# Top-32 attention and a mixture of depths on one core: the 32nd score found from a bound and an exact count, with a general way behind a branch

## The chip, the core and the metric

The program runs on one core of one Trainium2 chip. A core has a matmul engine (PE, whose weight loads are listed as PEld), a vector engine (DVE), an activation engine (ACT), a general engine (POOL) and a queue engine that issues most DMAs (SP). The metric is the device time of one execution in microseconds (us), the median of several runs.

## The reference

The inputs are fixed: the reference draws them after seeding its generator with 0. There are 8 batches, 8 heads, 576 tokens and 64 values per head.

```python
scores = scale * np.matmul(q, k.transpose(0, 1, 3, 2))          # scale = 1/8
kth = np.partition(scores, -32, axis=-1)[..., -32:-31]
scores = np.where(scores >= kth, scores, -1000000000.0)
attn = np.exp(scores - np.max(scores, axis=-1, keepdims=True))
attn = attn / (np.sum(attn, axis=-1, keepdims=True) + 1e-09)
x = np.matmul(attn, v)                       # -> (batch, token, 8 heads * 64 = 512)
# mixture of depths, per batch
s = x @ w_gate
top = the 128 tokens of the highest s
out = x;  out[top] = x[top] + sigmoid(s[top]) * (relu(x[top] @ w1) @ w2)
```

Each of the 8 x 8 x 576 = 36,864 rows of scores has 576 scores, and its 32nd greatest decides which scores count.

## The kernel before

**Tiles and units.** The queries of a head lie in four full tiles of 128 rows and a last one of 64. The work is cut into 160 units, 20 to a batch: a pair of heads (`hp`, 0 to 3) on a tile of queries (`t`, 0 to 4). A unit with `t` below 4 has two score tiles of 128 rows, one per head. A unit with `t` = 4 has one score tile that holds both heads' 64 rows. So there are 288 score tiles, each 128 rows by 576 scores.

**One unit.** `scores` multiplies on PE into PSUM (`ps`) and ACT copies the products to `sc`. `top_k` finds the 32nd score on DVE in four rounds: each round takes the 8 greatest (MAX8, tiles `first` and `best`), and between rounds a MATCH_REPLACE8 (with a small MATCH_VALUE_LOAD ahead of it) strikes them out into `left`. `weigh` makes `shift` on POOL, the exponentials `e` on ACT, a mask with the 32nd score on POOL and the product `p` on POOL. `turn` transposes `p` on PE (tiles `ptr` and `small`), ACT copies that to `pT`. `values` multiplies `pT` with `v` on PE into another part of `small`; a column of ones in `v` gives the sum of the weights. ACT copies the result to `xs`. After the four pairs of heads of a tile, `normalise` divides (DVE, then POOL writes `x`) and `gates` makes the tokens' gate scores (DVE, tile `prod`).

**Mixture.** When a batch's attention is done, `mixture` ranks its tokens (`tied`, on DVE), picks 128 with one-hot matmuls (`xe_ps`, `extra_ps`), runs the two layers (`h_ps`, `y_ps`) and adds the result to `out` with an indirect DMA that POOL issues. It is a generator; one step of it goes into each unit of the next batch.

**Order.** The order on PE, DVE, ACT and POOL is the order in which the code is written: the class `InOrder` records every operation of the main loop, so that nearly all of them carry line 33 in the profile, and they are told apart by tiles. The loop runs over n. While DVE does `top_k` for unit n, PE makes the scores of n + 1, the values of n - 2, and turns the weights of n - 1. The loads of q, k and v of the next batch (`load_qkv`, eight steps of transposes on PE and copies on ACT) go between the last units of a batch; SP issues their DMAs.

Of the kernel before, what the change touches and what calls it, by code (L numbers as in the profile page):

```python
# [15 lines left out]
# Below every score: what match_replace puts in place of the values already taken.  # L16
LOWEST = -3.0e38
TOP_K = 32
CAP = 128
# Full tiles of 128 tokens; token 4 * p + j sits on partition p of tile j, so that  # L20
# a partition's four tokens are contiguous in memory. The last 64 tokens are tile J.
# [3 lines left out]
class InOrder:  # L25
    """An engine whose instructions stay in the order in which they are written."""
# [10 lines left out]
def kernel(  # L37
# [29 lines left out]
    ldpool = ctx.enter_context(tc.tile_pool(name="ld", bufs=2))  # L67
    kqpool = ctx.enter_context(tc.tile_pool(name="kq", bufs=2))
    scpool = ctx.enter_context(tc.tile_pool(name="sc", bufs=6))
    wkpool = ctx.enter_context(tc.tile_pool(name="wk", bufs=4))  # L70
    stats = ctx.enter_context(tc.tile_pool(name="stats", bufs=12))
    ppool = ctx.enter_context(tc.tile_pool(name="p", bufs=3))
    ptpool = ctx.enter_context(tc.tile_pool(name="pt", bufs=4))
# [11 lines left out]
    # The place of each token in its sequence, and the row of slots 0 .. CAP-1.  # L85
# [8 lines left out]
    # before[p, t, c] = 1 where the token of column c comes before token (p, t):  # L94
    # of tokens with the same gate score, the earlier one is taken first.
# [24 lines left out]
    # v with a column of ones: the product with it is the softmax's denominator.  # L120
# [22 lines left out]
    def room_for_qkv(b):  # L143
        """q and k transposed, [(h d), pair of heads, token]; v as [token, head, tile, d]."""
        qT = kqpool.tile([P, NHP, S], FP32, name="qT")
        kT = kqpool.tile([P, NHP, S], FP32, name="kT")
        return qT, kT, vbufs[b % 2]

    def load_qkv(b, qT, kT, vt):
        """In 2 * NHP steps, k and q of a pair of heads; each asks for the next one's rows."""  # L150

        def fetch(src, hp, name):
            rows = ldpool.tile([P, NT, 2, D], FP32, name=name)
            for hh in range(2):
                nc.sync.dma_start(
                    out=rows[:, 0:J, hh, :],
                    in_=src[b, 2 * hp + hh, 0:JP, :].rearrange("(p j) d -> p j d", j=J),
                )
            nc.sync.dma_start(
                out=rows[0:R, J, :, :],  # L160
                in_=src[b, 2 * hp : 2 * hp + 2, JP:S, :].rearrange("h p d -> p h d"),
            )
            return rows
# [4 lines left out]
            for src, dst, name in ((k, kT, "kin"), (q, qT, "qin"))  # L168
        ]
        fetched = {}  # L170
        for i, (src, dst, hp, name) in enumerate(todo):
# [5 lines left out]
            for c in range(J):  # L177
# [15 lines left out]
                in_=v[b, i, 0:JP, :].rearrange("(p j) d -> p j d", j=J),  # L193
            )
            nc.sync.dma_start(out=vt[0:R, i, J, 0:D], in_=v[b, i, JP:S, :])
            yield

    def top_k(scs):
        """Of each tile's rows, the greatest score and the least of the TOP_K greatest."""
        cur, left, first = list(scs), {}, {}  # L200
        for r in range(TOP_K // 8):
            best = {}
            for i in range(len(scs)):
                best[i] = stats.tile([P, 8], FP32, name="best" if r else "first")
                dve.max(best[i], cur[i])
            first = first or best
            if r < TOP_K // 8 - 1:
                for i in range(len(scs)):
                    if r == 0:
                        left[i] = wkpool.tile([P, S], FP32, name="left")  # L210
                    dve.match_replace(left[i], best[i], cur[i], LOWEST)
                    cur[i] = left[i]
        return [(first[i][:, 0:1], best[i][:, 7:8]) for i in range(len(scs))]

    def heads_of(t):
        """Of each score tile of a pair of heads: its heads and their first rows.

        Rows of a score tile are queries: of one head in a full tile, and of both
        heads, one below the other, in the last tile.
        """  # L220
        return [[(0, 0), (1, R)]] if t == J else [[(0, 0)], [(1, 0)]]

    def scores(t, hp, qT, kT):
        """The pair's score tiles; two heads' products go to banks of their own."""
# [11 lines left out]
        scs = []  # L236
        for ps in pss:
            sc = scpool.tile([P, S], FP32, name="sc")
            act.copy(
                out=sc.rearrange("p (u s) -> p u s", u=2), in_=ps[:, :, 0:HALF]  # L240
            )
            scs.append(sc)
        return scs

    def weigh(scs, tops):
        """exp(scale * (score - greatest)) where a score is among its row's TOP_K, else 0."""
        weights = []
        for sc, (top, kth) in zip(scs, tops):
            shift = stats.tile([P, 1], FP32, name="shift")
            pool.tensor_scalar_mul(shift, top, -scale)  # L250
            e = ppool.tile([P, S], FP32, name="e")
            act.activation(e, sc, AF.Exp, bias=shift, scale=scale)
            p = ppool.tile([P, S], FP32, name="p")
            pool.tensor_scalar(
                out=p, in0=sc, scalar1=kth, scalar2=None, op0=ALU.is_ge
            )
            pool.tensor_tensor(p, p, e, ALU.mult)
            weights.append(p)
        return weights

    def turn(weights):
        """The weights transposed, [key, chunk of keys, query]."""
        small = ps_small.tile([P, 512], FP32, name="small")
        turned = []
        for i, p in enumerate(weights):
            pT = ptpool.tile([P, NT, P], FP32, name="pT")
            tr = ps_tr.tile([P, 512], FP32, name="ptr")
            for c in range(J):
                pe.transpose(
                    tr[:, c * P : (c + 1) * P], p[:, c * P : (c + 1) * P], ident  # L270
                )
            pe.transpose(small[0:R, i * P : (i + 1) * P], p[:, JP:S], ident)
            act.copy(
                out=pT[:, 0:J, :], in_=tr.rearrange("p (c i) -> p c i", c=J)
            )
            act.copy(out=pT[0:R, J, :], in_=small[0:R, i * P : (i + 1) * P])
            turned.append(pT)
        return turned, small

    def values(t, hp, turned, small, vt, xs):  # L280
        """The weights' product with v, and their sums, into the heads' columns of xs."""
        n = R if t == J else P
        for pT, heads in zip(turned, heads_of(t)):
            for hh, r in heads:
                for c in range(NT):
# [3 lines left out]
                        pT[0:rows, c, r : r + n],  # L289
# [9 lines left out]
    def normalise(n, xs, x):  # L299
        den = stats.tile([P, H], FP32, name="den")  # L300
# [11 lines left out]
    def route(gate, rank):  # L312
        """Each token's rank by gate score, [token, tile]."""
# [15 lines left out]
        for t in range(NT):  # L329
# [3 lines left out]
            tied = modpool.tile([P, S], FP32, name="tied", tag="scratch", bufs=2)  # L333
# [18 lines left out]
    def mixture(b, x, gate):  # L352
        """In steps, that go between those of the next batch's attention."""
# [3 lines left out]
        # What goes with a token to its slot: its row of out, and sigmoid(gate).  # L357
# [3 lines left out]
        for t0, t1, n in ((0, J, P), (J, NT, R)):  # L361
            dve.tensor_scalar_add(
                out=extra[0:n, t0:t1, 0], in0=tok_i[0:n, t0:t1], scalar1=float(b * S)
            )
            # exp(88) is finite, and its reciprocal below the least normal number.
# [71 lines left out]
        gy = modpool.tile([P, HD], FP32, name="gy", bufs=2)  # L437
        act.activation(gy, ps, AF.Copy, scale=g)
        # Every token has its x in out by then; a slot's token gets g * y on top.
# [8 lines left out]
    def gates(t, x, gate):  # L448
        n = R if t == J else P
        prod = modpool.tile([P, S], FP32, name="prod", tag="scratch", bufs=2)  # L450
# [11 lines left out]
    def store(b, x):  # L462
        nc.sync.dma_start(
            out=out[b, 0:JP, :].rearrange("(p j) n -> p j n", j=J), in_=x[:, 0:J, :]
        )
        nc.sync.dma_start(out=out[b, JP:S, :], in_=x[0:R, J, :])

    # Attention's units: a pair of heads on a tile of queries. While the vector
    # engine finds the top scores of unit n, the tensor engine makes the scores of
    # n + 1, the values of n - 2 and turns the weights of n - 1. The mixture of a  # L470
    # batch goes between the first units of the next one, and the loads of the batch
    # after that between the last.
    units = [(b, t, hp) for b in range(B) for t in range(NT) for hp in range(NHP)]
    per_batch = NT * NHP
    load_from = per_batch - 1 - 2 * NHP
    qkv = {0: room_for_qkv(0)}
# [5 lines left out]
    for n in range(-1, len(units) + 3):  # L482
# [8 lines left out]
        if n < 0:  # L491
            continue
# [32 lines left out]
    for _ in mixing:  # L525
        pass
# [33 lines left out]
```

## Time and profile before

| | |
|---|---|
| median of 3 runs | 1800.72 us (1799.33 to 1802.34) |
| profiled execution: span from the first to the last instruction | 1801.2 us |
| profiled execution's own time | not given beside its span, which lies 0.5 us above the median |
| DVE busy | 1552.2 us (86%), 3281 instructions |
| PE busy, weight loads | 1432.4 us (80%), 1114.2 us (62%) |
| POOL busy | 1052.5 us (58%) |
| ACT busy | 687.1 us (38%) |
| mean granted PE clock | 0.687 of full speed |

A group of instructions is printed as line, engine, operation, tiles written and read, shape and count, then the busy time in all and the mean in ns of one, then the idle time ahead of the group and what ended it. A timeline row has start, duration, engine, operation, tiles, shape and count, and in brackets the idle time before it. A row of the view by stages has the busy time of each engine in a stretch, the granted clock of PE and the DMA share.

### The profile page before, as it was taken

The numbers are of one execution on the slowest core, as the hardware profiler recorded it, in microseconds if no ns is written. First come the engines' busy times: TensorE is split into PE (matmuls) and PEld (weight loads), VectorE is DVE, ScalarE is ACT, GpSimd is POOL, SyncE is SP. The second block draws the span as 40 slices with busy tenths as digits, with TensorE's granted clock in tenths as the row PEclk, the third lists the DMA queues.
The fourth block names the chain that finished last, engine by engine and source line by source line (L and its number), as shares of the span: only waits on it lengthen the run. The fifth ranks groups of instructions, "written<-read, shape, count | busy, mean of one in ns | idle before, by whom it ended". The sixth has DMA issues, their size and how long they took to land.

```text
span 1801.2 us, 22598 instructions
## 1 busy us (share of the span) xinstructions
PE 1432.4 (80%) x7320; PEld 1114.2 (62%) x7320; DVE 1552.2 (86%) x3281; ACT 687.1 (38%) x1505; POOL 1052.5 (58%) x931
## 2 busy tenths in 40 slices
PE   5888777897778977789778897688876988769875
PEld 3667556575566756667557675576655866557554
DVE  7999798888988889887998879987799878998872
ACT  3444433344333443334433344333443334433330
POOL 5767465565656655556655566555665556655660
PEclk8766666857567575776757766577665767658767
DMA  7101200012000120001200112001120011000000
GB/s 196 35 5 29 70 3 1 13 27 73 1 1 13 27 73 1 0 13 29 71 1 1 19 28 66 1 1 20 30 63 1 1 19 37 4 1 1 7 24 9
DMA packets 120486, 45.77 MB, mean 25 GB/s; under 512 B 116144, under 2 KB 116144, under 8 KB 119344
## 3 DMA queue, kind: packets, MB, share of 16 engines
q1 hardware_dynamic: 119216, 42.23, 9.2%
q0 software_dynamic: 1152, 2.10, 0.9%
q8 instruction: 58, 0.95, 0.2%
q14 instruction: 60, 0.49, 0.1%
HBM read 32.77 MB, written 11.53 MB: 25 GB/s over the span
## 4 chain that ended last, share of the span: by engine, by line
DVE 42%; PE 27%; POOL 15%; issue 13%; ACT 3%; DMA 0%; POOLq 0%; SPq 0%; ACTq 0%; DVEq 0%
DVE left L33 15%; DVE best L33 15%; POOL p L33 13%; PE small L33 11%; DVE first L33 5%; PE ptr L33 4%; PE ps L33 4%; DVE tied L33 4%; PE h_ps L33 3%; PE tr L33 2%; PE xe_ps L33 1%; POOL shift L33 1%; DVE prod L33 1%; POOL x L33 1%; ACT e L33 1%
## 5 line engine op out<-in xcount | busy, mean ns | idle before, releaser
L33 POOL TENSOR_SCALAR p<-sc,best 128x576 f32<-128x576 f32 x288 | 526.0, 1827 | 211.3 <-DVE best L33 159.5
L33 DVE MAX8 best<-left 128x8 f32<-128x576 f32 x864 | 613.8, 746 | 4.4
L33 PEld LDWEIGHTS small<-v,pT 128*128 128x128 f32 (+3 forms) x3200 | 510.3, 237 | 138.5 <-issue 71.0
L33 PE MATMUL small<-v,pT 128*128 128x65 f32 (+3 forms) x3200 | 579.3, 336 | 2.1 <-ACT pT L33 2.1
L33 POOL TENSOR_TENSOR p<-p,e 128x576 f32<-128x576 f32 x288 | 407.2, 1414 | 282.7 <-ACT e L33 266.3
L33 PE MATMUL ptr<-ident,p 128*128 128x128 f32 x1152 | 279.1, 387 | 284.6 <-POOL p L33 284.5
L33 DVE MATCH_REPLACE8 left<-best,left 128x576 f32<-128x576 f32 x576 | 423.2, 741 | 0.0
L33 PEld LDWEIGHTS ptr<-ident,p 128*128 128x128 f32 x1152 | 187.7, 195 | 333.2 <-POOL p L33 320.1
L33 ACT ACTIVATE e<-sc,shift 128x576 f32<-128x576 f32 x288 | 223.4, 776 | 412.9 <-POOL shift L33 412.7
L33 PE MATMUL ps<-kT,qT 64*128 64x288 f32 (+1 forms) x1280 | 294.8, 583 | 1.1 <-ACT qT L33 1.1
L33 DVE MAX8 first<-sc 128x8 f32<-128x576 f32 x288 | 202.8, 740 | 75.0 <-ACT sc L33 74.9
L33 ACT COPY pT<-ptr 128x512 f32<-128x512 f32 x288 | 170.2, 591 | 221.6 <-PE ptr L33 221.4
L33 DVE MATCH_REPLACE8 left<-first,sc 128x576 f32<-128x576 f32 x288 | 211.6, 741 | 0.0
L33 PEld LDWEIGHTS ps<-kT,qT 64*128 64x128 f32 (+1 forms) x1280 | 159.7, 250 | 58.9 <-issue 16.1
L33 ACT COPY sc<-ps 128x576 f32<-128x576 f32 x288 | 169.0, 631 | 19.0 <-PE ps L33 18.0
L33 POOL TENSOR_TENSOR x<-xs,rden 128x512 f32<-128x512 f32 (+1 forms) x40 | 41.8, 1046 | 150.0 <-DVE rden L33 148.1
L33 ACT COPY xs<-small 128x130 f32<-128x130 f32 (+1 forms) x160 | 43.4, 271 | 178.0 <-PE small L33 177.9
L33 PE MATMUL small<-ident,p 128*64 128x128 f32 x288 | 108.8, 378 | 0.4 <-ACT pT L33 0.4
L33 DVE TENSOR_SCALAR den<-xs 128x8 f32<-128x8 f32 (+1 forms) x40 | 6.9, 171 | 81.4 <-ACT xs L33 81.4
L33 POOL TENSOR_SCALAR shift<-first 128x1 f32<-128x1 f32 x288 | 75.2, 261 | 1.1 <-DVE first L33 1.1
L33 ACT COPY pT<-small 64x128 f32<-64x128 f32 x288 | 74.9, 260 | 0.0
L33 PE MATMUL h_ps<-xeT,w 128*128 128x128 f32 x512 | 72.2, 309 | 0.4 <-DVE g L33 0.4
(54 smaller groups left out, 831.2 us busy)
## 6 DMA issues: line engine op xcount, KB each, us to landing
kin<-in_k_dram SPq DMA_DIRECT2D x64, 128.0 KB, 2.8
qin<-in_q_dram SPq DMA_DIRECT2D x64, 128.0 KB, 2.8
v<-in_v_dram SPq DMA_DIRECT2D x64, 128.0 KB, 2.6
out_dram<-x SPq DMA_DIRECT2D x8, 1024.0 KB, 4.4
w<-in_moe_w_dram SPq DMA_DIRECT2D x2, 2048.0 KB, 9.0
kin<-in_k_dram SPq DMA_DIRECT2D x32, 32.0 KB, 2.4
qin<-in_q_dram SPq DMA_DIRECT2D x32, 32.0 KB, 2.5
v<-in_v_dram SPq DMA_DIRECT2D x64, 16.0 KB, 2.3
```

Source lines behind the costliest of these rows:

```text
L33: return lambda *a, **kw: self._tc.keep_in_program_order(fn(*a, **kw))
```

## The change

**The 32nd score.** Instead of four rounds of MAX8 over 576 scores, the new `bound` folds a row to its 288 pairwise maxima (score i with score i + 288), splits them into two halves of 144, and takes the 16 greatest of each half, `a1..a16` and `b1..b16`, by MAX8, a masking multiply and MAX8 again. The bound is the greatest of min(a8, b16), min(a9, b15), ..., min(a16, b8), so at least 24 scores of the row are at or above it. `part` gives every score a sign against the bound (its upper 16 bits) on ACT and adds the signs up into `below`, an exact count. POOL multiplies the scores with their signs into `y`: scores at or above the bound become negative. `pick_kth` takes one MAX8 of `y`, the eight greatest scores below the bound, and picks among them the 32nd of the row by the count: with c scores at or above the bound it is the (32 - c)th of the eight, which exists when c lies from 24 to 31. With any other c nothing is picked, and `seen` keeps a 0 for that row.

**Weights.** ACT makes Relu(kth - score) times 2^90 into `z`, POOL subtracts it from the scores, PE transposes, and the exponential is taken when ACT moves the transposed scores out of PSUM (no maximum is subtracted). The loop is one unit deeper: `values` is at n - 3, `turn` at n - 2, `pick_kth` at n - 1, `bound` and `part` at n.

**The branch.** At the end, `least` is the minimum over `seen` (every row's bound and 32nd score) and `most` the maximum over the softmax sums. Where in any partition `least` is not above 1e-16 or `most` not below 1e6, `unsure` is positive, and every engine then runs `general`: a loop over the 8 batches that loads q, k, v anew, finds the 32nd score by the four rounds of before, and writes `out` and the mixture again.

**Buffers.** Pools get fewer or more buffers: loads 3 under one tag (before: 2 each for q and k), `sc` 4 (of twice the size), work tiles 2, statistics 6, `pT` 2 (of twice the size), scratch 1.

```diff
+    def bound(n, sc, at):
+        w = HALF // 2
+        m = wkpool.tile([P, 2, 2, w], FP32, name="m", bufs=1)
+        best = stats.tile([P, 2, 2, 16], FP32, name="best")
+        for i in range(n):
+            dve.tensor_tensor(
+                m[:, i, :, :].rearrange("p u s -> p (u s)"),
+                sc[:, i, 0:HALF], sc[:, i, HALF:S], ALU.max)
+            for u in range(2):
+                dve.max(best[:, i, u, 0:8], m[:, i, u, :])
+            for u in range(2):
+                dve.scalar_tensor_tensor(out=m[:, i, u, :], in0=m[:, i, u, :],
+                    scalar=best[:, i, u, 7:8], in1=m[:, i, u, :],
+                    op0=ALU.is_lt, op1=ALU.mult)
+            for u in range(2):
+                dve.max(best[:, i, u, 8:16], m[:, i, u, :])
+        pairs = stats.tile([P, 2, 9], FP32, name="pairs")
+        dve.tensor_tensor(pairs[:, 0:n, :], best[:, 0:n, 0, 7:16],
+                          best[:, 0:n, 1, 15:6:-1], ALU.min)
+        dve.tensor_reduce(out=seen[:, 0, at : at + n], in_=pairs[:, 0:n, :],
+                          axis=mybir.AxisListType.X, op=ALU.max)
+    def part(i, sc, at, sides, below):
+        act.activation(sides[:, i, :], sc[:, i, :], AF.Sign,
+            bias=seen[:, 0, at + i : at + i + 1].bitcast(BF16)[:, 1:2],
+            scale=-(1.0 + 2.0**-23), accum_out=below[:, i : i + 1])
+    def pick_kth(n, y, below, at):
...
+        for i in range(n):
+            dve.max(next8[:, i, :], y[:, i, :])
+            dve.scalar_tensor_tensor(out=hit[:, i, :], in0=place,
+                scalar=below[:, i : i + 1], in1=next8[:, i, :],
+                op0=ALU.is_equal, op1=ALU.mult,
+                accum_out=seen[:, 1, at + i : at + i + 1])
+        dve.tensor_scalar_mul(kth[:, 0:n], seen[:, 1, at : at + n], BIG)
+        return kth
...
     for n in range(-1, len(units) + 4):
...
+            pss = multiply(t, hp, *qkv[b][0:2])                    # unit n + 1
+        if is_unit(n - 2):
+            for i in range(tiles_of(n - 2)):
+                act.activation(z[:, i, :], sc[:, i, :], AF.Relu,
+                               bias=kth[:, i : i + 1], scale=-BIG)
+                pool.tensor_tensor(z[:, i, :], sc[:, i, :], z[:, i, :], ALU.subtract)
+        if pss is not None:
+            scs[n + 1] = keep(pss)
+        if is_unit(n - 3):
+            values(t, hp, *turned.pop(n - 3), qkv[b][2], xs)
+        if is_unit(n):
+            bound(tiles_of(n), scs[n], first_tile[n])
+        for i in range(2):
+            if is_unit(n) and i < tiles_of(n):
+                part(i, scs[n], first_tile[n], sides, below)
+                pool.tensor_tensor(y[:, i, :], scs[n][:, i, :], sides[:, i, :], ALU.mult)
+            if is_unit(n - 2) and i < tiles_of(n - 2):
+                turn(i, z, tr, small)
+                act.activation(pT[:, 0:J, i, :],
+                    tr.rearrange("p (c i) -> p c i", c=J), AF.Exp, scale=scale)
...
+        if is_unit(n - 1):
+            kths[n - 1] = pick_kth(tiles_of(n - 1), *masked.pop(n - 1), first_tile[n - 1])
...
+    dve.tensor_reduce(out=least, in_=seen, axis=mybir.AxisListType.XY, op=ALU.min)
+    dve.tensor_reduce(out=most, in_=sums, axis=mybir.AxisListType.XY, op=ALU.max)
...
+    def general_weights(n, sc):
+        p = wkpool.tile([P, 2, S], FP32, name="p", tag="z")
+        for i in range(n):
+            cur, tops = sc[:, i, :], []
+            left = wkpool.tile([P, 2, S], FP32, name="left", tag="y")
+            for r in range(TOP_K // 8):
+                tops.append(stats.tile([P, 8], FP32, name=f"top{r}"))
+                nc.vector.max(tops[-1], cur)
+                if r < TOP_K // 8 - 1:
+                    nc.vector.match_replace(left[:, 0, :], tops[-1], cur, LOWEST)
+                    cur = left[:, 0, :]
+            nc.vector.tensor_scalar_mul(shift, tops[0][:, 0:1], -scale)
+            e = wkpool.tile([P, S], FP32, name="e", tag="m", bufs=1)
+            nc.scalar.activation(e, sc[:, i, :], AF.Exp, bias=shift, scale=scale)
+            nc.vector.scalar_tensor_tensor(out=p[:, i, :], in0=sc[:, i, :],
+                scalar=tops[-1][:, 7:8], in1=e, op0=ALU.is_ge, op1=ALU.mult)
+        return p
+    def general(b, row0):
...
+        for _ in load_qkv(of(q), of(k), of(v), qT, kT, vt):
+            pass
+        for t in range(NT):
+            for hp in range(NHP):
+                p = general_weights(w, keep(multiply(t, hp, qT, kT)))
+                for i in range(w):
+                    turn(i, p, tr, small)
+                    nc.scalar.copy(...)                                  # pT
+                nc.scalar.copy(...)                                      # pT, last 64 keys
+                values(t, hp, pT, small, vt, xs)
+            normalise(rows, xs, x[0:rows, t, :], den)
+            gates(t, x, gate)
+        store(out[bass.ds(b, 1)].rearrange("o s n -> (o s) n"), x)
+        for _ in mixture(row0, x, gate):
+            pass
+    with tc.If(nc.values_load(unsure[0:1, 0:1]) > 0):
+        with tc.For_i(0, B) as b:
+            general(b, row0)
+            nc.vector.tensor_scalar_add(out=row0, in0=row0, scalar1=float(S))
```

## The prediction

> **What bounds the kernel now.** I read the page first (busy time, then the chain that ended last), then the groups, then the order of time.
>
> ```profile
> span 1801.2 us, 22598 instructions
> ...
> DVE 42%; PE 27%; POOL 15%; issue 13%; ACT 3%; DMA 0%; POOLq 0%; SPq 0%; ACTq 0%; DVEq 0%
> ...
> L33 DVE MAX8 best<-left 128x8 f32<-128x576 f32 x864 | 613.8, 746 | 4.4
> L33 POOL TENSOR_TENSOR p<-p,e 128x576 f32<-128x576 f32 x288 | 407.2, 1414 | 282.7 <-ACT e L33 266.3
> ```
>
> DVE leads the chain, and its MAX8 group is idle for 4.4 us in all: DVE waits for nobody inside a unit. In the order of time two units start 9.65 us apart:
>
> ```profile
> 303.20 1.41 DVE L33 MAX8 first<-sc 128x8 f32<-128x576 f32 x2
> ...
> 312.85 1.40 DVE L33 MAX8 first<-sc 128x8 f32<-128x576 f32 x2
> ```
>
> That is 8 MAX8 at 0.66 (two take 1.41 to 1.33, as the next starts before the end) and 6 strikes at 0.73: 9.65. A one-tile unit takes 5.62 (starts at 864.51 and 870.13). A batch of 16 x 9.65 + 4 x 5.62 = 177 us takes 222 us (the `first` rows of two batches, 426.3 and 648.2); the 45 us left are the mixture's and the gates' DVE work and DVE's waits, of which three groups carry most:
>
> ```profile
> DVE den L33 <- ACT xs L33: 81.4, 15, 8.9
> DVE first L33 <- ACT sc L33: 74.9, 16, 7.4
> DVE row_i L33 <- PE extra_ps L33: 51.9, 8, 8.1
> ```
>
> **First question: does the branch run?** It decides more than any duration. Its condition depends on data alone, and the reference's inputs are fixed, so I worked it out on them by arithmetic: all 36,864 rows of q k^T, columns in the kernel's order, the bound formed as `bound` does. The count c of scores at or above the bound is 24 in 16,277 rows, 25 in 12,471, 26 in 5,152, and falls off to 41. In 147 rows it is above 31, in every batch (11 to 23 rows each). There `place` meets no count, `hit` adds up to 0, `least` is 0 and `unsure` positive. The reason is the split: the two lists hold 16 each, and when more than 16 of the 24 greatest pair maxima fall into one half (chance 2 x 3.2% for 24 fair coins), the best pair left is min(a16, b8), and too many scores lie above it. So I take the general way as run: time = new main loop + eight turns of `general`.
>
> **The main loop.** Removed per full tile: 4 MAX8 and 3 strikes on 576. Added, uncovered on DVE, (N + overhead) from rows: TENSOR_TENSOR on 288, 0.46 (STT on 576 takes 0.82: 0.60 of stream at 576 elements and 0.2 fixed, so 0.30 + 0.16 here); four MAX8 on 144 at 0.21 to 0.30 (MAX8 on 576: 0.66, of it 0.60 stream); two STT at 0.29 to 0.36. With their dependences 1.9 us. Two tiles, `pairs` and the reduction (0.2 each, by `rden` 128x8, 203 ns): 4.3. `pick_kth`: two MAX8 at 0.78, two `hit` at 0.2, `kth` 0.2: 2.2. So 6.5 us for 9.65, if nothing collides.
>
> But STT and TENSOR_TENSOR read two SBUF tiles, and POOL now does nothing but TENSOR_TENSOR: `y` and `z`, four per unit. The trace has that pair:
>
> ```profile
> 260.97 1.64 POOL L33 TENSOR_TENSOR p<-p,e 128x576 f32<-128x576 f32 x1
> ...
> 261.28 1.94 DVE L33 SCALAR_TENSOR_TENSOR tied<-gate_row,gate,before 64x576 f32<-64x576 f32 x1
> ...
> 1760.74 0.82 DVE L33 SCALAR_TENSOR_TENSOR tied<-gate_row,gate,before 128x576 f32<-128x576 f32 x1 [0.77 <-ACT gate_row L33]
> ```
>
> With POOL idle (1760.74) STT takes 0.82. Beside a POOL TENSOR_TENSOR that began first it takes 1.94: it waits 1.12, to 0.2 before POOL's end, and POOL's op is 0.23 longer than its 1.41. So a POOL op keeps DVE's two-tile ops out for about 1.15. The ends: 0 waits (6.5 per unit), or four of 1.15 (11.1). Laid out by hand: `y` of tile 0 stops the second `hit` (0.4), `y` of tile 1 stops `kth` or the next fold (1.1), `z` stops the first masking STT (0.9), the second `z` the next one (1.1). I take 3.5, so 10.0 per unit, because a two-tile op comes on DVE every 0.2 to 0.8 us. One-tile units: 3.6 + 2 x 0.85 = 5.3.
>
> The Trainium skill (SBUF — State Buffer, "Who interferes with whom") says of such a pair that the second to issue fully blocks until the first finishes. The row above agrees for POOL's TENSOR_TENSOR; beside POOL's one-input mask the trace has STT at 0.79 and 1.19, so there the row, not the rule, holds. By the rule the main loop keeps its 10.0, without it 6.5, and about 450 us of main loop lie between.
>
> ACT per unit: two copies 1.2, two Relu and two Sign by `e` (0.78; Sign's sum 0 to 0.2 more), two Exp 0.6, the small Exp 0.37, `xs` 0.27: 6.3 to 6.7, under DVE's 10.0. Sign waits for `bound`; behind it queue Exp and the next Relu, and POOL waits for it; one unit of depth covers that. PE's work is unchanged: at the half clock 2.3 (`ps`) + 5.1 (values) + 2.0 (turns) = 9.4, also under 10.0; if DVE were faster, PE is next. The extra depth should cover two of the three waits above, so I lower the 45 us to 30 (both ends: 15 and 45). SP's and POOL's queues have DMAs with a unit to spare. Sum: 11 to the first MAX8; first batch 160 + 21 + 10 = 191; seven at 160 + 21 + 30 = 211; tail 62 (49 now, one unit of depth, the closing check): 1741 us, near the present time. No row shows the branch's read and jump; I bound it by 0 and 10 us.
>
> **The general way.** Here nothing is ahead: PE's order is scores, turns, values, and only then the next unit's scores, so DVE waits a full round trip. PE is idle half of each period, and such stretches run at the half clock: even the stretch below, with PE busy 9.82 of 10.50, was granted 0.50.
>
> ```profile
> 899.50:910.00 10.50, 9.82 (x42) 7.89 (x40) 10.50 (x23) 4.53 (x11) 6.70 (x7) 0.50 0.00 1
> ...
> 456.86 2.38 PE L33 MATMUL ps<-kT,qT 64*128 64x288 f32 x8
> 459.17 5.10 PE L33 MATMUL small<-v,pT 128*128 128x65 f32 x20
> ...
> 864.51 0.76 DVE L33 MAX8 first<-sc 128x8 f32<-128x576 f32 x1
> ```
>
> Full unit, step by step: four rounds on two tiles 9.65 and a `shift` 0.1; STT 0.8; then, as there is one `e` buffer, the second tile's `shift` 0.15, its exponential 0.8 and its STT 0.85 in a row (the waits between in them): 12.4 by here. Then the second turn until ACT can copy 1.15, copies 0.6 and 0.35, values 5.1, scores 2.35, ACT copy 0.65, handovers 0.1: 10.3. Together 22.7 us. One-tile unit: 5.6 + 0.85 + 1.15 + 0.85 + 3.0 + 2.4 + 0.65, less overlap: 14.3. Of a batch: 16 x 22.7 + 3 x 14.3 + 6.5 = 413 to its last weights. Ahead of it the loads, not overlapped: 24 DMAs of k and q at 0.6 of SP's time and 12 of v at 0.55 (SP rows: two in 1.22, one in 0.54), 21 us, landing 2.8, the last transposes and the first scores 5.5: 29. Behind it what the end of the trace shows from the last `p` (1752.35) to 1801.2: 49. The loop's turn, which no row shows: 4, between 0 and 10. One turn 495, eight 3960.
>
> The Trainium skill (TensorE: Matmul & The Clock Gate, Part 1) has the clock released after some 3.4 us of sustained work. By that rule values and scores would end at full clock and a unit would fall towards 20. The stretch above contradicts it, so the sum stays with the row.
>
> **Sum.** 1741 + 3960 = 5700 us. It is made against a span of 1801.2, which is within 0.03% of the median of 1800.72; no correction.
>
> **Rivals.**
> - *Half the price (15%):* the general way runs at full clock (values 2.87, scores 1.24, turns 0.7 in the trace's fast stretches), 3.8 less per unit: 16 x 3.8 x 8 = 486 off, total 5215. Or the main loop has no collisions: 16 x 3.5 x 8 = 450 off, 5250. With both, 4765. Against: 0.50 in nearly dense stretches, and the 1.94.
> - *The loop costs more (14%):* loop ends that stop all engines, addresses worked out for each DMA on SP, v late: 550 per turn, 4400, total 6150.
> - *The branch isn't taken (4%), the other side:* if c stayed in 24 to 31 in every row, only the main loop counts: 1741, faster by 3%, with its own ends 1741 - 450 = 1290 and 1741 + 140 = 1880. It decides from zero rows out of 36,864; one is enough to run all eight turns. For it speaks only that my count could misread the fold; 147 rows leave no margin for rounding.
> - *Slower main loop alone:* 11.1 per unit adds 140; too small to matter beside the branch.
>
> **Numbers.** Forecast 67%, half price 15%, dearer loop 14%, no branch 4%. The forecast's own range is 5400 to 6000 (main loop -250/+140, loads and tail of a turn 10%). For 8 in 10, the range reaches into both neighbours: 5150 to 6200. Faster by over 0.2% (about what a measurement of this kernel can tell from no change) only without the branch and with a main loop below 1797: 0.03; within 0.2%: 0.01; slower: 0.96.
>
> **What would show it.** Right: rows at the general way's lines (L676 for MAX8 on 576, L678 for the strikes, L683 for `e`), in number what before had for all tiles: 1152, 864 and 288; eight equal periods of about 495 us after some 1740 us; PE clock near 0.5 in them; DVE idle about 10 us per unit before its first MAX8, waiting for `sc`; in the main loop STT and fold rows well above 0.4 us on average beside `y` and `z`. Wrong: no such rows (branch not taken), unit starts 7 us apart in the main loop (no collisions), or turns much shorter than 495.

## The result, and the profile after

The kernel after takes 5613.33 us (median of 4 runs, 5605.77 to 5621.93), the kernel before beside it 1801.53: 3.1158 times as long, with a 95% interval of 3.1114 to 3.1202. The forecast was 5700. The branch runs, and its eight turns fill 70% of the time. The profiled execution has a span of 5607.4 us, 0.1% under the median; all sums below are made against it. Of the runs below, one (1686.18 us, with the branch off) lay over 1.5% above the fastest of its kernel; it counts as slow and is left out.

The page of the kernel after, first its groups of the general way (line, engine, operation, tiles, shape and count, then busy time and mean ns, then the idle time ahead of the group and what ended it):

```profile
span 5607.4 us, 45277 instructions
...
L676 DVE MAX8 top<-sc 128x8 f32<-128x576 f32 x288 | 206.2, 753 | 1576.2 <-ACT sc L39 1574.7
...
L676 DVE MAX8 top<-left 128x8 f32<-128x576 f32 x864 | 614.3, 747 | 2.2
L683 ACT ACTIVATE e<-sc,shift 128x576 f32<-128x576 f32 x288 | 223.3, 775 | 1260.0 <-DVE shift L681 1260.0
```

The four rounds of MAX8 on 576 are there again, 288 + 864 = 1152, as many as the kernel before has. In the kernel before the first MAX8 of a unit waited 74.9 us in all for `sc`; here it has waited 1575 us. One period of the general way in the order of time, DVE and then PE (start, duration, engine, operation; in brackets the idle time before it):

```profile
2705.58 0.80 DVE L686 SCALAR_TENSOR_TENSOR p<-sc,top,e 128x576 f32<-128x576 f32 x1
...
2707.35 0.82 DVE L686 SCALAR_TENSOR_TENSOR p<-sc,top,e 128x576 f32<-128x576 f32 x1 [0.90 <-ACT e L683]
...
2718.23 1.42 DVE L676 MAX8 top<-sc 128x8 f32<-128x576 f32 x2 [10.06 <-ACT sc L39]
...
2740.59 0.76 DVE L676 MAX8 top<-sc 128x8 f32<-128x576 f32 x1 [10.06 <-ACT sc L39]
```

```profile
2706.53 1.09 PE L39 MATMUL ptr<-ident,p 128*128 128x128 f32 x4 [11.37 <-DVE shift L681]
...
2708.31 1.09 PE L39 MATMUL ptr<-ident,p 128*128 128x128 f32 x4 [0.48 <-DVE p L686]
...
2710.34 4.89 PE L39 MATMUL small<-v,pT 128*128 128x65 f32 x19 [0.72 <-ACT pT L718]
...
2715.24 2.23 PE L39 MATMUL ps<-kT,qT 64*128 64x288 f32 x7
```

DVE works, then PE works, and neither has anything of the next unit: turn, copy, values, scores and copy lie in the 10.06 us before each first MAX8. These units start 22.36 us apart.

Three stretches make the span. The main loop with its tail ends at 1671 us (the last indirect DMA of its mixture starts at 1669.21 and takes 1.58). The first MAX8 of the eight turns come at 1692.3, 2179.6, 2673.6, 3168.2, 3663.0, 4155.2, 4649.5 and 5141.2, so 487 to 495 us apart, mean 492.7. The last turn ends the span.

In the main loop the question was POOL's `y` and `z` beside DVE. The instructions of the helper's line in the kernel after (count, then ns least/median/greatest of one):

```profile
L39 DVE SCALAR_TENSOR_TENSOR m<-m,best x576: 348/360/3993, 12.4 to 1606.6; 128x144 f32<-128x144 f32 x192
...
L39 DVE TENSOR_TENSOR m<-sc x288: 398/446/1544, 11.4 to 1605.0; 128x288 f32<-128x288 f32 x144
...
L39 DVE SCALAR_TENSOR_TENSOR hit<-place,below,next x288: 225/228/1390, 30.9 to 1612.9; 128x8 f32<-128x8 f32 x144
...
L39 DVE TENSOR_SCALAR kth<-seen x160: 153/1193/1403, 32.2 to 1613.5; 128x2 f32<-128x2 f32 x128, 128x1 f32<-128x1 f32 x32
```

STT is short for SCALAR_TENSOR_TENSOR, and the TENSOR_TENSOR that writes `m` is the fold. Most STT, folds and `hit` are as short as the prediction costed them, and some take over 1 us longer; of the `kth` with two columns most are long. Their means, for the experiments below:

```profile
L39 DVE SCALAR_TENSOR_TENSOR m<-m,best 128x144 f32<-128x144 f32 x576 | 383.8, 707 | 0.0
...
L39 DVE TENSOR_TENSOR m<-sc 128x288 f32<-128x288 f32 x288 | 194.3, 675 | 26.7 <-ACT sc L39 26.7
...
L39 DVE TENSOR_SCALAR kth<-seen 128x2 f32<-128x2 f32 x128 | 116.7, 912 | 4.4
```

One of the long ones, in the order of time:

```profile
404.96 1.65 POOL L39 TENSOR_TENSOR y<-sc,sides 128x576 f32<-128x576 f32 x1 [1.50 <-ACT sides L39]
...
405.41 1.52 DVE L39 TENSOR_TENSOR m<-sc 128x288 f32<-128x288 f32 x1
...
408.99 0.43 DVE L39 TENSOR_TENSOR m<-sc 128x288 f32<-128x288 f32 x1
```

The fold that starts during a `y` ends 0.3 us after it; the one that starts with POOL idle takes 0.43.

### The profile page after: what moved, and what is told of

It reads as the page before. It is cut to its first block, busy times and chain, and to the rows that moved or that the text cites. A ratio compares the mean times of both kernels' runs of the same rounds, so it can differ in the third digit from the quotient of the medians.

```text
span 5607.4 us, 45277 instructions
## 1 busy us (share of the span) xinstructions
PE 3129.5 (56%) x14642; PEld 2409.5 (43%) x14642; DVE 3273.4 (58%) x7633; ACT 1601.8 (29%) x3329; POOL 920.1 (16%) x693
## 5 line engine op out<-in xcount | busy, mean ns | idle before, releaser
L39 PE MATMUL small<-v,pT 128*128 128x65 f32 (+3 forms) x6400 | 1319.5, 371 | 241.2 <-ACT pT L39 128.8
L39 PEld LDWEIGHTS small<-v,pT 128*128 128x128 f32 (+3 forms) x6400 | 1162.3, 268 | 504.5 <-ACT pT L718 184.9
L39 PE MATMUL ps<-kT,qT 64*128 64x288 f32 (+1 forms) x2560 | 685.8, 626 | 1.7 <-ACT qT L39 1.7
L676 DVE MAX8 top<-left 128x8 f32<-128x576 f32 x864 | 614.3, 747 | 2.2
L39 POOL TENSOR_TENSOR y<-sc,sides 128x576 f32<-128x576 f32 x288 | 372.7, 1308 | 551.6 <-ACT sides L39 523.5
L39 POOL TENSOR_TENSOR z<-sc,z 128x576 f32<-128x576 f32 x288 | 427.1, 1502 | 149.8 <-issue 105.4
L678 DVE MATCH_REPLACE8 left<-top,left 128x576 f32<-128x576 f32 x576 | 423.5, 742 | 0.0
L39 DVE SCALAR_TENSOR_TENSOR m<-m,best 128x144 f32<-128x144 f32 x576 | 383.8, 707 | 0.0
L39 DVE MAX8 best<-m 128x8 f32<-128x144 f32 x1152 | 297.0, 298 | 9.9
L39 PE MATMUL ptr<-ident,z 128*128 128x128 f32 x1152 | 258.3, 367 | 44.3 <-POOL z L39 41.7
## 6 DMA issues: line engine op xcount, KB each, us to landing
w<-in_moe_w_dram SPq DMA_DIRECT2D x2, 2048.0 KB, 10.1
```

What stands on the lines that cost most here:

```text
L39: return lambda *a, **kw: self._tc.keep_in_program_order(fn(*a, **kw))
L676: nc.vector.max(tops[-1], cur)
L678: nc.vector.match_replace(left[:, 0, :], tops[-1], cur, LOWEST)
```

## The experiments

### Does the data set off the branch, and what is the main loop worth alone?

```diff
-    with tc.If(nc.values_load(unsure[0:1, 0:1]) > 0):
+    with tc.If(nc.values_load(unsure[0:1, 0:1]) > 87):     # second run: > 86
```

> The branch asks for more than 87 unsure partitions in place of more than 0. By arithmetic on the fixed inputs the 147 rows with a count above 31 lie in 87 of the 128 partitions, so unsure is 87 and the general way is skipped; in this run those 147 rows get no 32nd score. My theory (these rows alone set off the branch, and the main loop is what the profile of after shows ahead of the general way, whose weights' store was issued at 1669 us): 1671 us and the end of the program, 1665 to 1690, about 7% under the kernel before. Rival 1 (something else sets it off, such as the row sums or a bound of zero, in more partitions): the general way still runs, 5610. Rival 2 (a branch not taken costs as much as its code loads or drains): above 1700.

Measured: 1674.06 us (median, 1659.6 to 1674.33), 0.9253 of before (0.9204 to 0.9301). At more than 86:

> The kernel after with the branch's condition at more than 86 unsure partitions. The run with more than 87 skipped the general way. By the arithmetic on the inputs 87 partitions hold a row with more than 31 scores at or above the bound, neither more nor fewer, so here it must run: 5607 us. Rival (fewer are unsure, so the arithmetic misreads the kernel's bound somewhere): skipped, 1674.

Measured: 5600.24 us in a single run. So `unsure` is 87, neither more nor less: as many partitions fail as the arithmetic named. The run without the general way has a span of 1672.6, and in the kernel after the main loop ends at 1671, so a branch not taken costs less than these runs tell apart. The fast way alone gains 7%; the general way costs 3940 us.

### Is it the bound alone? An exact 24th pair maximum

```diff
-    (two halves of 144: MAX8, masking STT, MAX8 each; best of the splits)
+            dve.tensor_tensor(m[:, i, :], sc[:, i, 0:HALF], sc[:, i, HALF:S], ALU.max)
+            for r in range(3):
+                dve.max(best[:, i, r, :], m[:, i, :])
+                if r < 2:
+                    dve.match_replace(m[:, i, :], best[:, i, r, :], m[:, i, :], LOWEST)
+        dve.tensor_reduce(out=seen[:, 0, at : at + n], in_=best[:, 0:n, 2, :], op=ALU.min, ...)
```

> The bound is the exact 24th greatest of the 288 pair maxima (three MAX8 on 288 with two strikes between them) in place of two lists of 16 and the best split between them. By arithmetic its count is 24 to 30 in all 36,864 rows, so unsure is 0 and the branch, at its old condition, is not taken. My theory: per tile the fold 0.45, three MAX8 at 0.37 and two strikes at 0.44 (half of 0.742 and a value load) take the place of fold, four MAX8 at 0.22 and two masking STT at 0.28; that is 0.5 us more uncovered per tile, but the strikes have one tile input and stood at 0.730 to 0.748 us in the profile of before with POOL at work beside them, so the STT group's excess (179 of 445 us over seven batches) goes: per batch 201 + 18 - 26 = 193, about 1600 us in all, 1560 to 1640. Rival 1 (strikes are held out by POOL too): 201 + 18 = 219 per batch, 1810. Rival 2 (POOL's stalls only move to the next two-tile instruction): 1690 to 1810. If the branch is taken all the same: over 5500.

Measured: 1768.23 us, 0.9786 of before (0.974 to 0.9833). The branch, at its old condition, is not taken: the split was the cause. This kernel beats before by 1.7 to 2.6%, but it is 170 us over its own expectation: 215 us per batch where 193 were expected. POOL doesn't hold the strikes out (0.443 us in the mean). The time also lies in the range of rival 2, and a little of it is that: in the mean `kth` with two columns rose from 0.912 to 1.049 us and the fold from 0.675 to 0.748, while `hit` fell from 0.427 to 0.388, some 27 us in all. What was mis-sized above all is the chain inside one tile, here in the order of time:

```profile
435.29 0.46 DVE L39 MAX8 best<-m 128x8 f32<-128x288 f32 x1
435.78 0.09 DVE L39 MATCH_VALUE_LOAD m<-best,m 128x8 f32 x1
435.86 0.44 DVE L39 MATCH_REPLACE8 m<-best,m 128x288 f32<-128x288 f32 x1
436.34 0.46 DVE L39 MAX8 best<-m 128x8 f32<-128x288 f32 x1
```

From MAX8 to the load 0.49, and from the load to the next MAX8 0.56: each starts 0.03 to 0.04 us after the end of the one that it needs, where in the kernel before, with two tiles in turn, two MAX8 of 0.75 take 1.41 together, so the second starts 0.08 before the first ends. Three MAX8 and two strikes at these distances take 2.6 us per tile for the 2.0 of the sum; 0.6 more on the 36 tiles of a batch are the 22 us that were missing. That led to the next run.

### Two tiles in turn, and `kth` by columns

```diff
-            (in the loop over tiles: three rounds on one tile, then on the other)
+        for r in range(3):
+            for i in range(n):
+                dve.max(best[:, i, r, :], m[:, i, :])
+            if r < 2:
+                for i in range(n):
+                    dve.match_replace(m[:, i, :], best[:, i, r, :], m[:, i, :], LOWEST)
...
-        dve.tensor_scalar_mul(kth[:, 0:n], seen[:, 1, at : at + n], BIG)
+        for i in range(n):
+            dve.tensor_scalar_mul(kth[:, i : i + 1], seen[:, 1, at + i : at + i + 1], BIG)
```

> The exact 24th pair maximum as in the run before, with two edits: the rounds of a unit's two tiles alternate (MAX8 of tile 0, MAX8 of tile 1, strike of tile 0, strike of tile 1) instead of one tile after the other, and kth is made by two one-column instructions in place of one with two columns. Theory for the shortfall of the run before (1768 where 1600 was expected): each MAX8 waited for the strike before it and each strike for its MAX8, 0.48 and 0.56 us from start to start where 0.37 and 0.42 were in the sum, 0.6 us per tile, 21 us per batch; alternated, they cost the sum's price: 1600. On top, kth by columns is not held out by POOL (one column 0.15 us, two columns 0.87 us in the mean there): if that stall vanishes, 15 us more per batch: 1480; if it moves to the fold behind it, nothing: 1600. Expected 1540, 1480 to 1610. Rival (POOL's stalls set the unit whatever the order): above 1700.

Measured: 1591.8 us, 0.8819 (0.8772 to 0.8866). Near 1600, at which the stall of `kth` only moves on. The alternated rounds were not run alone; the second edit alone, on the kernel after with the threshold at 87, shows how little it is worth there:

> The kernel after with the branch's threshold at 87 (147 rows get no 32nd score, as in the first run), and kth made by two one-column instructions instead of one with two columns. Its excess in the profile of after is 86 us over seven batches, 98 over eight. Theory A (the two-column form, not its place in the order, is what POOL holds out, and the stall does not come back): 1575. Theory B (two columns are held out, one is not, but the next fold takes over the wait for the end of the second y): kth at 0.15 us, the fold's mean up from 0.67 towards 1.0, 1630 to 1680. Rival (any instruction at this place waits): kth's two columns at 0.5 us or more each, 1675 or more. I hold B the likelier.

Measured: 1654.81 us, 0.9179 (0.9164 to 0.9195), so 19 us less than the median without the edit (5 to 20 less than its single runs), where `kth`'s excess was 98. Groups of that run:

```profile
L39 DVE SCALAR_TENSOR_TENSOR m<-m,best 128x144 f32<-128x144 f32 x576 | 403.4, 740 | 0.0
...
L39 DVE TENSOR_TENSOR m<-sc 128x288 f32<-128x288 f32 x288 | 209.3, 727 | 21.2 <-ACT sc L39 21.2
...
L39 DVE TENSOR_SCALAR kth<-seen 128x1 f32<-128x1 f32 x288 | 39.0, 149 | 1.1
```

`kth` is never late now (149 ns), and in its place the masking STT rose from 0.707 in the kernel after to 0.740 and the fold from 0.675 to 0.727: theory B, with 34 us found again at these two. So a hold that one instruction no longer waits out can be waited out by the next ones that POOL holds up; where the rest of the 98 went was not traced.

Next, the fold as an instruction that reads one tile:

```diff
-            dve.tensor_tensor(m[:, i, :], sc[:, i, 0:HALF], sc[:, i, HALF:S], ALU.max)
+            dve.tensor_reduce(out=m[:, i, :], op=ALU.max, axis=mybir.AxisListType.X,
+                in_=sc[:, i, :].rearrange("p (u s) -> p s u", u=2))
```

> As the run with alternated rounds, and the fold of the two halves is a TENSOR_REDUCE over one tile (576 read once, pairs the same) in place of a TENSOR_TENSOR over two. Price uncovered: about 0.66 us (one pass over 576, as MAX8 on 576) for 0.48. Theory (the fold's mean excess of 0.30 us, or 0.3 and the stall that kth handed on, is POOL's): 0.1 to 0.7 us per tile better, 4 to 25 us per batch: 1480 us, 1440 to 1560, where PE and ACT, which the run with one-input products on POOL shows at 1459, take over. Rival (the stall moves on to hit, which has two inputs too): equal to the run with alternated rounds or up to 30 us slower.

Measured: 1579.19 us, 0.8746 (0.8704 to 0.8788). It misses its range of 1440 to 1560, and the intervals of this run and the one before overlap, so the 13 us between them are not safely apart: the rival's "equal" fits. This is the fastest version run that computes what the reference asks: 12.5% under before, with all rows covered by the fast way. The fold no longer waits for POOL, but with one input it costs 0.748 us in the mean, about what it cost with its waits:

```profile
L39 DVE TENSOR_TENSOR m<-sc 128x288 f32<-128x288 f32 x288 | 209.7, 763 | 44.8 <-ACT sc L39 44.5
```

```profile
L39 DVE TENSOR_REDUCE m<-sc 128x288 f32<-128x576 f32 x288 | 205.2, 748 | 40.5 <-ACT sc L39 40.5
```

The first row is the run before, the second this run. `hit` and `tied` still wait, and the chain of this run is 47% DVE and 37% PE: DVE alone no longer sets it.

### POOL with one tile input

```diff
-    pool.tensor_tensor(z[:, i, :], sc[:, i, :], z[:, i, :], ALU.subtract)
+    pool.tensor_scalar(z[:, i, :], z[:, i, :], 0.0, None, ALU.mult)
-    pool.tensor_tensor(y[:, i, :], scs[n][:, i, :], sides[:, i, :], ALU.mult)
+    pool.tensor_scalar(y[:, i, :], scs[n][:, i, :], 1.0, None, ALU.mult)
```

> POOL's two products y and z become products with a constant (one tile input; y is a copy of the scores, z is zero, so the weights are not the reference's) and the branch's condition can't be met. DVE, ACT and PE have the same instructions. My theory (POOL's two-input instructions hold DVE's two-tile ones out, 445 us over seven batches in the profile of after): the masking STT falls from 0.70 to 0.36 us, the two-column kth from 1.19 to 0.16, hit from 0.43 to 0.23; DVE's unit would be 7 us, but PE at the half clock (9.4 per full unit) becomes the bound: about 1350 us, 1200 to 1500. Rival 1 (any POOL instruction that reads SBUF holds them out): no less than 1640. Rival 2 (DVE's excess is not POOL but its own dependences): 1660 to 1690.

Measured: 1459.49 us in a single run, 215 less than with the two-input products, though POOL is busy for longer (1.69 us per instruction for 1.40). Groups of that run:

```profile
L39 DVE SCALAR_TENSOR_TENSOR m<-m,best 128x144 f32<-128x144 f32 x576 | 230.5, 440 | 0.0
...
L39 DVE TENSOR_TENSOR m<-sc 128x288 f32<-128x288 f32 x288 | 137.8, 478 | 102.7 <-ACT sc L39 102.7
...
L39 DVE TENSOR_SCALAR kth<-seen 128x2 f32<-128x2 f32 x128 | 30.6, 239 | 4.4
```

Most of the collisions go with POOL's second input, as the theory says; some shorter ones stay (the masking STT has a mean of 0.440 us for a free 0.36). The edit gave 215 us, not the 450 of the rival "no collisions", and 1459 lies near the upper end of the expected range: the fold now waits 103 us for `sc`, for 27 in the kernel after, and the chain is 36% DVE, 35% PE, 12% ACT.

### The general way: the round trip, the clock, the one `e`

Scores one unit ahead:

```diff
+        todo = [(t, hp) for t in range(NT) for hp in range(NHP)]
+        sc = keep(multiply(*todo[0], qT, kT))
...
-                p = general_weights(w, keep(multiply(t, hp, qT, kT)))
+                this, u = sc, t * NHP + hp + 1
+                if u < len(todo):
+                    sc = keep(multiply(*todo[u], qT, kT))
+                p = general_weights(w, this)
```

> Only the general way changes: the scores of the next unit are multiplied and copied out of PSUM before the present unit's four rounds, one unit ahead. My theory (10.06 us of each 22.31 us period is DVE waiting for sc at the end of the round trip turn, copy, values, scores, copy): DVE runs through; a full unit falls to 12.0 (DVE busy 12.25 with some overlap, PE at the half clock 10.5 beside it), a one-tile unit from 14.3 to about 7.5; per turn 16 x 10.3 + 4 x 6.8 = 192 less, eight turns 1540 less: 4070 us, 3950 to 4250. Rival 1 (PE's own chain turns, values, scores at the half clock with ACT's copies in it is the real bound): 13 to 15 per unit, 4350 or more. Rival 2 (loads, gates and mixture of a turn grow because they were hidden in the idle time): 4300 and more.

Measured: 4313.51 us in a single run, 1300 less than after, 63 above the expected range. A full unit takes 12.42 us in the median, so the round trip is the cause of the 10.06. Rival 2 is not the reason for the miss, though 4313 lies in its range: from the last `p` of a turn to the next turn's first MAX8 this run takes 82.5 to 88.2 us, the kernel after 81.6 to 88.0. The rest of the forecast went to two places. The first unit of the second to fourth tile of queries takes 16.1 to 16.8, because `den` of the tile before stands among its rounds in DVE's queue and waits for the last values. DVE's waits in that run (us in all, times, longest):

```profile
DVE top L676 <- ACT sc L39: 584.5, 127, 56.6
DVE den L39 <- ACT xs L39: 157.5, 40, 5.3
```

And two of the three one-tile periods of a turn stayed near 12.5 instead of 7.5.

The clock: 7 matmuls of 128x512 for each tile in the gap of the general way, their result overwritten.

```diff
-                p = general_weights(w, keep(multiply(t, hp, qT, kT)))
+                sc = keep(multiply(t, hp, qT, kT))
+                trs = [ps_tr.tile([P, 512], FP32, name="ptr") for _ in range(w)]
+                for tr in trs:
+                    for _ in range(7):
+                        pe.matmul(tr, ident, w2[:, 0, :], start=True, stop=True)
+                p = general_weights(w, sc)
...
-                    tr = ps_tr.tile([P, 512], FP32, name="ptr")
+                    tr = trs[i]
```

> The kernel after with 7 extra matmuls of 128x512 per tile in the general way, put between a unit's scores and its first turn, where PE is idle for 12.2 us; their result is overwritten by the turn. It asks whether PE's idle time is what keeps the clock at 0.50. Theory A (more array work raises the granted clock): the values fall from 4.89 to 2.9, the scores from 2.3 to 1.24, the turns from 1.09 to 0.63 twice; a full unit from 22.3 to 18 or 19: 5100 us. Theory B (the clock stays at half in such a mix whatever fills the gap): the extra matmuls take 0.85 each, 11.9 us, just as long as the gap, and the unit stays at 22.3 or gains up to 1: 5600 to 5750. Mixed windows: between.

Measured: 5205.71 us in a single run, 400 less than after for more work: theory A, though 106 us above its 5100. A full unit takes 19.87 us in the median, where 18 or 19 were expected; the clock is not full throughout (0.93 granted from 2300 to 2400 us, 0.50 in the kernel after). Stretches, of the kernel after and of this run (width, busy time of PE, PEld, DVE, ACT and POOL, then the granted clock):

```profile
2710.34:2717.40 7.06, 7.06 (x28) 5.78 (x28) 0.00 (x0) 0.27 (x1) 0.00 (x0) 0.50 0.00 0
```

```profile
2402.83:2422.10 19.27, 18.13 (x69) 9.98 (x69) 11.40 (x24) 5.04 (x10) 0.00 (x0) 1.00 0.00 0
```

The values and scores of a unit, 7.06 us of PE without a gap, stay at 0.50. With the wide matmuls ahead of them they run at 1.00: 19 value matmuls take 2.75 us there, for the 4.89 shown in the period above:

```profile
2417.56 2.75 PE L39 MATMUL small<-v,pT 128*128 128x65 f32 x19 [0.83 <-ACT pT L723]
```

Last, the `e` buffer. First each tile gets its own, then `shift` and `e` also move up behind the first MAX8:

```diff
-            e = wkpool.tile([P, S], FP32, name="e", tag="m", bufs=1)
+            e = left[:, 1, :]
```

> The general way's exponential e lies in the unused half of left, so each tile has its own; nothing else changes, and the second shift stays behind the first p in DVE's order. The prediction put 1.8 us per unit (0.15 and 0.8 and 0.85 in a row) down to the single e buffer. If the buffer is the cause: 1.0 us less per full unit, 128 units: 5480. If DVE's order alone is (shift of tile 1 after the p of tile 0): unchanged, 5600 to 5615. I hold the second the likelier now.

Measured: 5611.69 us in a single run, the full unit 22.31 as in the kernel after.

> As the run with two e buffers, and shift and exponential are issued right after the first MAX8 of each tile, so both e are ready long before p. DVE's chain loses the second shift 0.15 and the wait 0.90 for e. But the second turn on PE began only 0.48 us after the first turn's last matmul, so of the 1.05 us at most about 0.5 reaches the values: 0.5 per full unit, 5607 - 64 = 5540; if all of it reaches the end, 5475; if none (PE's turns set the time), 5600.

Measured: 5498.7 us in a single run, the full unit 21.65, so 0.66 us less, where 0.5 was expected at most. That is 84 of the 110 us by which the span is shorter than after's; the rest lies outside the units, and its cause is open. The second turn then follows the first at once, where 1.78 us lie between their starts in the kernel after:

```profile
2431.48 1.09 PE L39 MATMUL ptr<-ident,p 128*128 128x128 f32 x4 [11.43 <-DVE p L687]
...
2432.57 1.06 PE L39 MATMUL ptr<-ident,p 128*128 128x128 f32 x4
```

## Why the prediction was right

**The branch.** Right, and it carries the forecast: the arithmetic on 147 rows decided 3940 us, and the two thresholds show its count of partitions to the last one. The reason given, the split into two lists, is shown by the exact 24th maximum, which needs no branch. But the prediction's 2 x 3.2% is only the chance that the bound falls below the 24th maximum, some 2,360 rows; its own count has only 147, 0.4% of all rows, above 31.

**The main loop.** 1741 was forecast, 1671 came. The collisions were sized well: 3.5 us per full unit was taken, and the groups' means over their medians give 3.0 (masking STT 576 x 0.35, fold 288 x 0.23, `hit` 288 x 0.20, `kth` 128 x 0.74 with two columns' free 0.17, and 10 for `pairs`: 430 us over 288 tiles). `y` and `z` hold out `kth` too, which has one input; the prediction had `kth` wait for `y` without a reason. Full units with no other work on DVE start 10.1 us apart (median of 29), for 10.0. What was mis-sized is the term beside the units: the first batch took 193 us for 191, the next six 202 in the mean for 211, the last 198, so 30 us of extras should have been nearer 20. Its bounds of 15 and 45 held. From the last `kth` (1613.5) to 1671 the tail took 57 for 62.

**The general way.** 495 per turn was forecast, 492.7 came: 22.31 us per full unit for 22.7, 14.31 per one-tile unit for 14.3. Two misses cancelled, which is luck: in the second turn the stretch from the first MAX8 to the end of the last `p` took 406.4 for 413, and from there to the next turn's first MAX8 87.6 for 82 (2586.0 to 2673.6). In the latter, the loop's turn on SP took 5.0 (from the indirect DMA's end at 2636.83 to the first load at 2641.80) for 4, and the loads up to the first MAX8 31.8 for 29. No row of the kernel before shows the loop's turn; its 4 was a guess. The round trip of 10.3 came out at 10.06.

**The single `e`.** Right in size, wrong in cause. The 1.8 us in a row are there, but a second buffer changes nothing: DVE's order has the second `shift` behind the first `p`. And moved out of that order, only 0.66 of the 1.05 us (0.15 and 0.90) reaches the end, since part of it lay beside the first turn.

**The clock.** Right for this kernel, 0.50 to 0.52 in the general way, but the reason was too short. The prediction set a nearly dense stretch at 0.50 against the Trainium skill (TensorE: Matmul & The Clock Gate, Part 1), which has the clock released after some 3.4 us of sustained work. Here 7.06 us without a gap stay at 0.50, so not all that the profile shows as busy counts as such work. With 512-wide matmuls in the gap the clock is released. The kernel before runs the values at full clock behind matmuls of 128 columns (`h_ps` at 323.55, the values at 328.38 in 2.87 us), so 512 columns are not needed; what in them, or in the closed gap, does it, no run here separates. The rival at full clock, priced at 486 us, was one edit away: 403 came (spans 5607.4 and 5204.0).

**The rivals.** "No collisions" was priced at 450. POOL with one input, which still holds some instructions, brings 215, and by then PE and ACT have 47% of the chain. The prediction had PE at 9.4 us per unit and did not use it in that rival. "Branch not taken" would have given 1674, inside its 1290 to 1880 and near its 1741.

**In one line:** 1671 for 1741 is 70 of the 93 us by which 5700 lies above the span; the eight turns are the other 23.

## What to carry to other kernels

A fast way with an exact fallback is worth its gain times the chance that no row at all fails, less the fallback's cost times the chance that one does: where inputs are fixed, count the failing rows before anything else, and spend on the bound (here an exact 24th maximum in place of a split) before spending on speed. On DVE, let two tiles take turns in a chain of dependent instructions, and count, beside a POOL that reads two tiles, the instructions that need the second input; taking one of them away can hand its wait to the next. The loop written here as a fallback had no overlap until it was written in.

## What the runs showed of the hardware that was not expected

The holds can be counted in the traces: DVE instructions that start while a `y` or `z` runs on POOL (more than 0.15 us before its end), and of them those that take over 1.3 times their free duration. Beside POOL's TENSOR_TENSOR, in the kernel after, all 420 of the four commonest kinds with two tile inputs are held (STT 171, fold 78, `hit` 129, `tied` 42), by 0.8 us in the mean; in the two last versions of the bound none of 511 strikes and none of 103 one-tile folds. Beside POOL's one-input TENSOR_SCALAR it is 196 of 841, and by 0.36 us in the mean, and they end while POOL's instruction still runs. The Trainium skill (SBUF — State Buffer, "Who interferes with whom") has a DVE instruction with two SBUF inputs contend with a POOL instruction that reads SBUF, and whichever comes second fully blocked for the whole of the other: the first pair agrees, the last does not.

`kth` multiplies by a constant and has one tile input. In the kernel after 92 starts with two columns fell beside `y` or `z`, and all were held, by 1.04 us in the mean; the 8 with one column were not, nor any of 280 in the three runs that have that form throughout. The Trainium skill (VectorE: DVE Perf Modes, "Mode 2×_2P — use both read ports for one tensor") has such an instruction use both read ports where the outermost dimension longer than one is even, or odd and the same in source and destination. Two columns held agree with that, and one column has no such dimension. Two more instructions with one tile input bear it out: in those three runs all 50 `sums` (8 columns) and all 21 `extra` (4 columns) that start beside `y` or `z` are held. That it is this mode, no trace here shows.
